# The last product of a fused retention and MoE kernel: 1024 of its 2304 tokens by Strassen's seven products

## The chip, the cores and the metric

The kernel runs on one core of one Trainium2 chip. The metric is the device time of one execution in microseconds (us). Three executions of the kernel before took 803.22, 806.06 and 806.58 us; the median is 806.06.

TensorE (PE) multiplies: a matmul holds a 128x128 stationary operand, loaded by a weight load, and streams a moving operand of up to 512 columns past it into a PSUM bank. VectorE (DVE) and ScalarE (ACT) move and combine data, and SyncE (SP) issues the DMAs, each from one queue that is worked off in order.

## The reference

```python
def _moe2_ref(x, w_in, w_out, alpha):
    h = x @ w_in
    g = np.maximum(h, 0.0) + alpha * np.minimum(h, 0.0)
    return (g @ w_out).astype(np.float32)
...
    x = np.ascontiguousarray(attn_out.transpose(0, 2, 1, 3)).reshape(B * S, H * D)   # retention
    x = _moe_ref(x=x, **moe_kwargs)                                                  # ((x w1)(x w2)) w3 w_out
    return _moe2_ref(x=x, **moe2_kwargs)
```

There are 2304 tokens (B 4 by S 576). Only the last product, g @ w_out, matters here: g is 2304 x 2048, w_out is 2048 x 512, and the result goes to `out`. The inputs' weights are float64, and everything is computed in float32.

## The kernel before

Every float32 product is made of three matmuls in fp32r, a shorter float form: an operand x is split into a high part, `hi = cast(x)` on ACT, and a low part, `lo = x - hi` on DVE (`split`, lines 172 and 173), and the product is hi·hi + hi·lo + lo·hi. Both parts of the stationary side come first with `hi`, then `lo`, so the third matmul of each three needs the low part.

The stages are, in order: retention and the two products of x (line 179), the folding of w3 with w_out (line 630), the product y (line 816), h = y @ w_in by Strassen's seven products (`Group`, line 883), and the last product (line 1044). h is made in groups (p, j): p is a pair of blocks of 384 tokens (`W`), and j one of eight (`C1`) slices of 256 of the 2048 features. Each group leaves four tiles of g, which `keep` writes to DRAM as `gd[feature block, token block]`, 128 features by 384 tokens each.

The last product reads g back. It goes in 48 steps (j, b), j a slice of 256 features and b a block of 384 tokens:

```python
steps = [(j, b) for j in range(C1) for b in range(2)] + [(j, b) for b in range(2, NB) for j in range(C1)]
```

Blocks 0 and 1 go together in six PSUM banks, because the weights w_out (`wbc`, raw pieces `raw`, line 85) become ready only during this time: `ws.tick()` moves each piece of them on through ACT and DVE (lines 93 to 116). The blocks 2 to 5 follow one after another in three banks each. A step's work:

- `load_g(n + 3)` issues two loads of 192 KB on SP's queue into a tile `gr` (a ring of three buffers, so tile n + 3 waits until the split of tile n is done, line 945).
- `split_g(n + 1)` makes `gh` on ACT and `gl` on DVE (two buffers each, so the split of step n + 1 waits until PE has finished step n - 1).
- 18 matmuls of 512 columns (line 1044), with g as the stationary operand and w_out as the moving one.
- After a block's last step, `write` copies its banks to `ot` on DVE or ACT and issues the output's DMA on SP's queue.

PE, ACT and SP work in the order in which the program is written; DVE's order is set by a scheduler when the kernel is built. Each DMA on SP's queue also waits for the DMA eight places before it.

Of the kernel before, what the change touches and what calls it, by code (L numbers as in the profile page):

```python
# [23 lines left out]
C1 = DF1 // P  # L24
# [3 lines left out]
W = 384  # L28
NB = NT // W
# [3 lines left out]
def _f32(ap):  # L33
    return ap.bitcast(F32)
# [5 lines left out]
class Steps:  # L40
# [97 lines left out]
def retention_moe_kernel(ctx: ExitStack, tc, qk, kv, w_out1, w3t, w12, w_in, w_out2, alpha, c_row, c_pair, out):  # L138
    nc = tc.nc

    def pool(stack, name, bufs=1, **kw):
        return stack.enter_context(tc.tile_pool(name=name, bufs=bufs, **kw))
# [4 lines left out]
    raws = pool(ctx, "raws", bufs=3, side="left")  # L147
    tmp = pool(ctx, "tmp", bufs=2, side="left")
# [500 lines left out]
    xo = pool(ctx, "xo", bufs=8, side="left", reuse_waits="tile")  # L649
# [4 lines left out]
    def a_sum(name):  # L654
        return sums.tile([P, 1024], F32, tag="s", name=name)
# [13 lines left out]
    def home(q, u):  # L669

        n = q % 2 * 7 + u
        if n < 8:
            return in_wa(C1 + n, f"wu{q}_{u}")
        return hold.tile([P, 2, DM], F32R, tag=f"wu{n}", name=f"wu{q}_{u}")

    class Pairs:
# [25 lines left out]
        def step(self, n, s):  # L702
            w, j = self.w, self.ORDER[n]
            q, odd = j // 2, j % 2
            i0, i1 = 2 * n, 2 * n + 1
            if s == 0:
                w.load_until(i0 + 3)
                w._first(i0)
            elif s == 1:
                w._second(i0)  # L710
                w.load_until(i0 + 4)
                w._first(i1)
            elif s == 2:
# [122 lines left out]
    py.close()  # L836


    back = pool(ctx, "back", side="right", reuse_waits="tile")
    pg = ExitStack()  # L840
    gp = pool(pg, "gp", side="right", bufs=2, reuse_waits="tile")

    def fetch(q, u):
# [20 lines left out]
    gd = {}  # L864
# [68 lines left out]
            self.product(self.b3, "S4", "B22", False)  # L933
            self.from_sum(self.b3, self.u2, 0, 1)

    NM = W // P
    steps = [(j, b) for j in range(C1) for b in range(2)] + [(j, b) for b in range(2, NB) for j in range(C1)]
    loaded, ready, accs = {}, {}, {}

    def load_g(n):  # L940
        if n < len(steps):
            j, b = steps[n]
            t = loaded[n] = gr.tile([P, 2, W], F32, tag="gr", name=f"gr{n}")
            for m in range(2):
                nc.sync.dma_start(out=t[:, m], in_=gd[2 * j + m, b])

    def split_g(n):
        if n < len(steps):
            x = loaded.pop(n)
            ready[n] = tuple(ghl.tile([P, 2, W], F32R, tag=f"g{m}", name=f"g{m}{n}") for m in "hl")  # L950
            split(ready[n][0], ready[n][1], x)

    def write(b, i):
        ot = raws.tile([P, 512], I64, tag="raw", name=f"ot{b}_{i}").bitcast(F32)[:, 0:DM]
        if i % 2:
            nc.scalar.copy(ot, accs[b][i])
# [67 lines left out]
    flush()  # L1024


    pg.close()
    used = 0
    for n, (j, b) in enumerate(steps):
# [5 lines left out]
        if b not in accs:  # L1035
            accs[b] = [bank((used + i) % 8, f"o{b}_{i}") for i in range(NM)]
            used += NM
        h, l = ready.pop(n)
        for i in range(NM):
            ic = slice(i * P, (i + 1) * P)  # L1040
            for m in range(2):
                wh, wl = wbc[2 * j + m]
                for q, (x, y) in enumerate(((h, wh), (h, wl), (l, wh))):
                    nc.tensor.matmul(accs[b][i], x[:, m, ic], y, start=(j == 0 and m == 0 and q == 0),  # L1044
                                     stop=(j == C1 - 1 and m == 1 and q == 2))
            if j == C1 - 1:
# [82 lines left out]
```

## Time and profile before

| | |
|---|---|
| three executions | 803.22, 806.06, 806.58 us |
| the profiled execution | 803.67 us, of which the span is 801.9 us |
| PE busy | 787.3 us, 98% of the span |
| DVE, ACT busy | 497.7 us (62%), 348.6 us (43%) |
| last product on PE | from 599.98 us to the end |

The stretches of the last product, by the profile's windows:

| us | PE busy | DVE busy | ACT busy | granted clock |
|---|---|---|---|---|
| 600 to 640 | 38.61 of 40 | 37.45 | 25.98 | 1.00 |
| 640 to 680 | 40.00 of 40 | 13.62 | 9.80 | 1.00 |
| 680 to 760 | 80.00 of 80 | 21.66 | 17.75 | 1.00 |
| 760 to 802 | 38.33 of 42 | 10.30 | 7.88 | 1.00 |

Busy time is time in which an instruction of the engine ran. Matmuls overlap, so a busy PE says only that it did not wait; what a matmul costs is the distance from one start to the next. The granted clock is TensorE's, 1.00 for its upper level of 2.4 GHz, 0.50 for 1.2 GHz.

### The profile page before, as it was taken

Reading aid. Unit: us, or ns where it says so; the run is one execution under the profiler, and the core shown is the slowest. Engines: PE = TensorE matmul, PEld = TensorE weight load, DVE = VectorE, ACT = ScalarE, POOL = GpSimd, SP = SyncE. Lnnn points to the kernel's source line nnn. Section 1 sums busy time; section 2 is a strip of 40 time slices with the busy share of each in tenths; the row PEclk is TensorE's granted clock in tenths of the full one; section 3 lists DMA queues with packets and bytes.
Section 4 is the critical chain, followed back from the end, with each engine's and each line's share of the span. In section 5 each row is a group of like instructions: output and inputs, shape, how many; then the busy total and the mean of one; then the engine's idle time right before and its main releaser. Section 6 shows DMA issues by size and latency. Waiting matters only on the chain.

```text
span 801.9 us, 12688 instructions
## 1 busy us (share of the span) xinstructions
PE 787.3 (98%) x4768; PEld 694.1 (87%) x4768; DVE 497.7 (62%) x895; ACT 348.6 (43%) x648; POOL 0.2 (0%) x4
## 2 busy tenths in 40 slices
PE   7999999999999999999999999999999999999998
PEld 4778888888888988999999999999987888888886
DVE  4796785325477788988843677587899933222232
ACT  3553562231255565656514465465666622222121
POOL 0000000000000000000000000000000000000000
PEclk8999999999999999999999999999999999999999
DMA  9844931571366659899916925225557635344341
GB/s 345 344 158 125 356 135 54 165 249 54 123 193 183 198 197 336 296 388 407 387 63 221 352 101 196 108 96 202 182 196 239 218 99 177 106 132 138 99 136 41
DMA packets 81341, 156.24 MB, mean 195 GB/s; under 512 B 9600, under 2 KB 57728, under 8 KB 81280
## 3 DMA queue, kind: packets, MB, share of 16 engines
q1 hardware_dynamic: 81280, 155.43, 55.7%
q8 instruction: 37, 0.61, 0.3%
q14 instruction: 24, 0.20, 0.1%
HBM read 104.02 MB, written 51.38 MB: 194 GB/s over the span
## 4 chain that ended last, share of the span: by engine, by line
PE 89%; DVE 5%; DMA 2%; ACT 1%; issue 1%; SPq 1%; ACTq 0%; DVEq 0%
PE ps L179 25%; PE o L1044 23%; PE h L883 18%; PE y L816 12%; PE pw L630 5%; PE o L342 2%; PE sc L287 2%; DMA raw<-in_w_dram 1%; PE o L333 1%; PE st L302 1%; DMA gr<-gd 0%; DVE gl L173 0%; DVE xs L349 0%; DMA xs<-x2d 0%; DVE rt L291 0%
## 5 line engine op out<-in xcount | busy, mean ns | idle before, releaser
L179 PE MATMUL ps<-xh,w 128*128 128x512 f32 (+1 forms) x640 | 186.0, 372 | 2.0 <-ACT w L112 1.6
L1044 PE MATMUL o<-wb,gh 128*128 128x512 f32 x576 | 177.6, 389 | 0.9 <-ACT gh L172 0.9
L179 PEld LDWEIGHTS ps<-xh,w 128*128 128x128 f32 x640 | 116.0, 189 | 23.6 <-ACT w L112 1.8
L1044 PEld LDWEIGHTS o<-wb,gh 128*128 128x128 f32 x576 | 108.1, 188 | 23.8 <-ACT gh L172 1.4
L179 PE MATMUL ps<-xl,w 128*128 128x512 f32 (+1 forms) x320 | 118.0, 369 | 0.0
L1044 PE MATMUL o<-wb,gl 128*128 128x512 f32 x288 | 112.3, 390 | 0.4 <-DVE gl L173 0.4
L173 DVE TENSOR_TENSOR gl<-gr,gh 128x768 fp32r<-128x768 f32 x48 | 46.0, 958 | 99.9 <-ACT gh L172 99.8
L816 PE MATMUL y<-yab,wp 128*128 128x384 f32 x576 | 100.0, 334 | 0.0
L816 PEld LDWEIGHTS y<-yab,wp 128*128 128x128 f32 x576 | 99.9, 188 | 0.1
L172 ACT CAST gh<-gr 128x768 fp32r<-128x768 f32 x48 | 40.2, 838 | 115.9 <-PE o L1044 112.6
L179 PEld LDWEIGHTS ps<-xl,w 128*128 128x128 f32 x320 | 60.4, 189 | 9.8 <-DVE xl L173 0.3
L1044 PEld LDWEIGHTS o<-wb,gl 128*128 128x128 f32 x288 | 54.1, 188 | 12.3 <-DVE gl L173 1.3
L895 DVE SCALAR_TENSOR_TENSOR g<-m,al,g 128x384 f32<-128x384 f32 x48 | 29.7, 618 | 48.9 <-ACT g L894 45.8
L883 PE MATMUL h<-xT,wv 128*128 128x384 f32 x288 | 54.9, 334 | 1.5 <-DVE g L901 1.5
L883 PE MATMUL h<-xT,wu 128*128 128x384 f32 x288 | 55.0, 335 | 0.5 <-ACT h L908 0.3
L883 PEld LDWEIGHTS h<-xT,wv 128*128 128x128 f32 x288 | 50.3, 188 | 1.8 <-DVE g L901 1.8
L108 DVE CUSTOM_DVE_ANT_0 a<-a,b 128x1024 uint16<-128x1024 uint16 x72 | 49.5, 688 | 3.5
L883 PEld LDWEIGHTS h<-xT,wu 128*128 128x128 f32 x288 | 50.2, 188 | 1.1 <-ACT h L908 0.6
L487 ACT CAST ab<-f 128x512 fp32r<-128x512 f32 (+1 forms) x40 | 23.1, 577 | 63.1 <-DVE f L491 54.5
L103 DVE TENSOR_SCALAR a<-a 128x512 f32<-128x512 f32 x72 | 30.4, 422 | 25.7 <-ACT a L93 25.4
L491 DVE TENSOR_TENSOR f<-f,ps 128x512 f32<-128x512 f32 (+1 forms) x40 | 25.3, 632 | 31.6 <-PE ps L179 31.3
L630 PE MATMUL pw<-wo,w 128*128 128x512 f32 x192 | 44.1, 390 | 0.0
(95 smaller groups left out, 1007.5 us busy)
## 6 DMA issues: line engine op xcount, KB each, us to landing
gd<-g SPq DMA_DIRECT2D x96, 192.0 KB, 1.9
gr<-gd SPq DMA_DIRECT2D x96, 192.0 KB, 2.6
abd<-ab SPq DMA_DIRECT2D x32, 512.0 KB, 4.3
raw<-in_w_out_dram SPq DMA_DIRECT2D x24, 512.0 KB, 3.7
yab<-abd SPq DMA_DIRECT2D x24, 384.0 KB, 7.9
raw<-in_w_dram SPq DMA_DIRECT2D x16, 512.0 KB, 7.1
raw<-in_w3t_dram SPq DMA_DIRECT2D x16, 512.0 KB, 4.1
rawi<-in_w_in_dram SPq DMA_DIRECT2D x16, 512.0 KB, 6.3
```

The costliest lines, as they stand in the source:

```text
L103: nc.vector.tensor_scalar(out=a, in0=a, scalar1=self.LEAST, scalar2=self.MOST, op0=ALU.max, op1=ALU.min)
L108: nc.vector.tensor_tensor(out=a.bitcast(I32), in0=a.bitcast(I32), in1=b, op=ALU.add)
L172: nc.scalar.copy(hi, src)
L173: nc.vector.tensor_tensor(out=lo, in0=src, in1=_f32(hi), op=ALU.subtract)
L179: nc.tensor.matmul(ps, a, bb, start=(n == 0), stop=(n == last))
L487: nc.scalar.copy(t[:, 0], f)
L491: nc.vector.tensor_tensor(out=f, in0=f, in1=pss[1], op=ALU.mult)
L630: nc.tensor.matmul(acc[i], a[:, ic], bb, start=(k == 0 and n == 0), stop=(k == C1 - 1 and n == 2))
L816: nc.tensor.matmul(ys[o], wpc[c][a][:, oc], yab[b, c][:, bb], start=(c == 0 and i == 0), stop=(c == C1 - 1 and i == 2))
L883: nc.tensor.matmul(ps, a[:, x, ks], b[:, y, k], start=(fresh and n == 0), stop=(n == 5), skip_group_check=True)
L895: nc.vector.scalar_tensor_tensor(out=g, in0=r, scalar=neg[:, c:c + 1], in1=g, op0=ALU.mult, op1=ALU.add)
L1044: nc.tensor.matmul(accs[b][i], x[:, m, ic], y, start=(j == 0 and m == 0 and q == 0), stop=(j == C1 - 1 and m == 1 and q == 2))
```

## The change

The 2304 tokens of the last product are divided in three. The first 1024 (blocks 0 and 1, and 256 tokens of block 2) go together in eight banks, in 24 steps (three for each j). The next 256 (the other 128 of block 2, and 128 of block 3) follow in two banks, in 16 steps of six matmuls. The last 1024 go in four rounds of 256 tokens by Strassen's seven products: for each j, g's 256 x 256 piece is four quadrants of 128 x 128 (A11 to A22) and four sums of them (S1 to S4, `add_two`), w_out's 256 x 512 piece is four quadrants of 128 x 256 and four sums (T1 to T4, `t_sums`), and seven products of three matmuls with 256 columns each take the place of eight.

```diff
-    steps = [(j, b) for j in range(C1) for b in range(2)] + [(j, b) for b in range(2, NB) for j in range(C1)]
+    TOGETHER = ((0, 0, W), (1, 0, W), (2, 0, 256))
+    THEN = ((2, 256, P), (3, 0, P))
+    steps = [(j, *x) for y in (TOGETHER, THEN) for j in range(C1) for x in y]
...
+                nc.sync.dma_start(out=t[:, m], in_=gd[2 * j + m, b][:, at:at + w])
...
+    gs = pool(ctx, "gs", side="right", bufs=3, reuse_waits="tile")
+    go = pool(ctx, "go", side="right", bufs=3, reuse_waits="tile")
...
+    def t_sums(j):
+        for m, w in enumerate((w0, w1)):
+            h, l = wbc[2 * j + m]
+            nc.vector.tensor_tensor(out=w, in0=_f32(h), in1=_f32(l), op=ALU.add)
+        less(t12[:, :HW], w0[:, HW:], w0[:, :HW])
+        less(t12[:, HW:], w1[:, HW:], t12[:, :HW])
+        def rest():
+            less(t34[:, :HW], w1[:, HW:], w0[:, HW:])
+            less(t34[:, HW:], w1[:, :HW], t12[:, HW:])
...
+            for t, cols, src in places:
+                nc.scalar.copy(t[:, 0, cols], src)
+            for t, cols, src in places:
+                nc.vector.tensor_tensor(out=t[:, 1, cols], in0=src, in1=_f32(t[:, 0, cols]), op=ALU.subtract)
...
+    def load_two(u):
+        t = sums_of[u] = gs.tile([P, 2, 7, P], F32, tag="gs", name=f"gs{u}")
+        for i in range(2):
+            j = (2 * u + i) % C1
+            for m in range(2):
+                for h in range(2):
+                    nc.sync.dma_start(out=t[:, i, PLACE[f"A{h + 1}{m + 1}"]],
+                                      in_=gd[2 * j + m, b][:, at:at + P])
...
+        for out, x, y, how in (("S1", "A21", "A22", ALU.add), ("S3", "A11", "A21", ALU.subtract),
+                               ("S2", "S1", "A11", ALU.subtract), ("S4", "A12", "S2", ALU.subtract)):
+            nc.vector.tensor_tensor(out=a[out], in0=a[x], in1=a[y], op=how)
+    def high_part(n):
+            nc.scalar.copy(x[:, 0], sums_of[n // 2][:, n % 2])
+    def low_part(n):
+            nc.vector.tensor_tensor(out=x[:, 1], in0=sums_of[n // 2][:, n % 2], in1=_f32(x[:, 0]),
...
+    ahead = [lambda: load_two(0), lambda: load_two(1), lambda: load_two(2), None, lambda: add_two(0), None,
+             lambda: high_part(0), lambda: add_two(1), lambda: low_part(0), None, lambda: high_part(1), None]
...
+        else:
+            t_steps.tick(w * 0.0032)
         load_g(n + 3)
         split_g(n + 1)
+        if n >= len(steps) - len(ahead):
+            step = ahead.pop(0)
...
+    for n in range(n_tail):
+        high_part(n + 2)
+        low_part(n + 1)
+        if n % 2:
+            add_two(n // 2 + 2)
+            load_two(n // 2 + 3)
+        for a, op, k, half in PRODUCTS:
+            for i, (y, z) in enumerate(((0, 0), (0, 1), (1, 0))):
+                nc.tensor.matmul(ps, a[:, y], b[z], start=(opens and j == 0 and i == 0),
```

After each round of eight n, six more operations on ACT and DVE combine the four banks' halves into two tiles of the output. The changed kernel's lines 947, 1092, 1102, 1107, 1112, 1146 and 1169 are the loads `gr`, the loads `gs`, the sums S, the high and the low parts `go`, the plain matmuls and those of the seven products.

**On PE**, the last rows of the program, before (o: a bank of the output; wb: a piece of w_out; gh, gl: the parts of g):

```order
L1044 MATMUL o5_2_7677<-wb14_6854,gh47_7818 128x512 x2
L1044 MATMUL o5_2_7677<-wb14_6854,gl47_7819 128x512
L1044 MATMUL o5_2_7677<-wb15_6886,gh47_7818 128x512 x2
L1044 MATMUL o5_2_7677<-wb15_6886,gl47_7819 128x512
```

and of the change (q: a bank; go: both parts of the quadrants and sums of g; t123, t4: those of the sums T):

```order
L1169 MATMUL q24_0_8359<-wb14_6845,go31_8500 128x256 x3
L1169 MATMUL q24_0_8359<-t123_7_7495,go31_8500 128x256 x3
L1169 MATMUL q24_1_8360<-t123_7_7495,go31_8500 128x256 x3
L1169 MATMUL q24_2_8361<-t123_7_7495,go31_8500 128x256 x3
L1169 MATMUL q24_2_8361<-t4_6_7391,go31_8500 128x256 x3
L1169 MATMUL q24_3_8362<-wb15_6877,go31_8500 128x256 x6
```

Each n of the last 1024 tokens is 21 matmuls of 256 columns.

**On SP's queue**, before, where step 28 of the 48 is worked on (gr: the tiles of g, two loads each):

```order
L945 DMA gr31_7347<-gd14_3_5799 128x384
L945 DMA gr31_7347<-gd15_3_5733 128x384
L945 DMA gr32_7372<-gd0_4_5761 128x384
L945 DMA gr32_7372<-gd1_4_5870 128x384
L945 DMA gr33_7397<-gd2_4_5857 128x384
L945 DMA gr33_7397<-gd3_4_5948 128x384
```

and of the change, at its step 28, the fifth of the sixteen short ones (gs: the four quadrants of two slices):

```order
L947 DMA gr31_7365<-gd6_3_5451 128x128
L947 DMA gr31_7365<-gd7_3_5404 128x128
L1092 DMA gs0_7372<-gd0_3_5217 128x128 x2
L1092 DMA gs0_7372<-gd1_3_5170 128x128 x2
L1092 DMA gs0_7372<-gd2_3_5295 128x128 x2
L1092 DMA gs0_7372<-gd3_3_5248 128x128 x2
L947 DMA gr32_7398<-gd8_2_5425 128x128
L947 DMA gr32_7398<-gd9_2_5516 128x128
```

Eight loads now stand between the loads of two steps; the same follows between gr32 and gr33 (gs1) and between gr33 and gr34 (gs2).

**On ACT**, of the change, at the end of the 24 steps of the eight banks (gh24 and gh25: the high parts of the first two short steps; ot: a copy of a finished bank; the L1065 rows: the high parts of sums T):

```order
L172 CAST gh24_7272<-gr24_7183 128x2x128
L959 COPY ot2_0_1_7291<-o2_0_1_6583 128x512
L1065 CAST t123_5_7297<-t12_5_7230 128x512
L1065 CAST t123_5_7297<-t34_5_7294 128x256
L1065 CAST t4_4_7221<-t34_5_7294 128x256
L172 CAST gh25_7307<-gr25_7235 128x2x128
```

The copy of the last bank of the eight, and three casts, stand ahead of the cast that the second short step waits for. On DVE the four sums of gs0 stand between gl31 and gl32, those of gs1 between gl32 and gl33, and those of gs2 between gl33 and gl34.

## Rows read from the trace of the kernel before

**Rows 1.** The page of the kernel before: busy time by engine, and the chain that ended last

```profile
PE 787.3 (98%) x4768; PEld 694.1 (87%) x4768; DVE 497.7 (62%) x895; ACT 348.6 (43%) x648; POOL 0.2 (0%) x4
...
PE ps L179 25%; PE o L1044 23%; PE h L883 18%; PE y L816 12%; PE pw L630 5%; PE o L342 2%; PE sc L287 2%; DMA raw<-in_w_dram 1%; PE o L333 1%; PE st L302 1%; DMA gr<-gd 0%; DVE gl L173 0%; DVE xs L349 0%; DMA xs<-x2d 0%; DVE rt L291 0%
```

**Rows 2.** The chain that ended last, its end: start us, us, what

```profile
614.88 183.46 PE o L1044 x808
...
798.36 0.69 DVE ot L958
```

**Rows 3.** PE in order of time, its 256-wide matmuls: start us, us

```profile
255.78 0.28 PE L179 MATMUL ps<-xl,w 128*128 128x256 f32 x1
...
258.06 0.40 PE L179 MATMUL ps<-xh,w 128*128 128x256 f32 x2
...
258.42 0.40 PE L179 MATMUL ps<-xh,w 128*128 128x256 f32 x2
...
278.58 0.28 PE L179 MATMUL ps<-xh,w 128*128 128x256 f32 x1
```

**Rows 4.** Groups of matmuls and weight loads by form: busy us, mean ns

```profile
L1044 PE MATMUL o<-wb,gh 128*128 128x512 f32 x576 | 177.6, 389 | 0.9 <-ACT gh L172 0.9
...
L179 PE MATMUL ps<-xh,w 128*128 128x256 f32 x128 | 23.2, 283 | 0.0
...
L1044 PEld LDWEIGHTS o<-wb,gl 128*128 128x128 f32 x288 | 54.1, 188 | 12.3 <-DVE gl L173 1.3
```

**Rows 5.** SyncE's queue in order of time, a burst of eight loads

```profile
488.13 3.64 SPq L997 DMA_DIRECT2D xs<-x2d  x8
```

**Rows 6.** SyncE's issues of the loads gr: duration ns min/median/max

```profile
L945 SPq DMA_DIRECT2D gr<-gd x96: 319/431/1068, 584.9 to 780.0; - x96
```

**Rows 7.** DMA issues: xcount, KB each, us from issue to landing

```profile
gr<-gd SPq DMA_DIRECT2D x96, 192.0 KB, 2.6
...
out_dram<-ot SPq DMA_DIRECT2D x18, 256.0 KB, 2.0
...
per_pair<-const_pair_dram SPq DMA_DIRECT2D x4, 64.0 KB, 2.2
```

**Rows 8.** SyncE's queue in order of time, two loads of 64 KB

```profile
68.08 1.06 SPq L389 DMA_DIRECT2D per_pair<-const_pair_dram  x2
```

**Rows 9.** Groups on DVE and ACT by form: busy us, mean ns

```profile
L173 DVE TENSOR_TENSOR gl<-gr,gh 128x768 fp32r<-128x768 f32 x48 | 46.0, 958 | 99.9 <-ACT gh L172 99.8
...
L116 DVE TENSOR_TENSOR wb<-a,wb 128x512 fp32r<-128x512 f32 x16 | 11.0, 685 | 0.0
...
L724 DVE TENSOR_TENSOR s<-a 128x256 f32<-128x256 f32 x8 | 3.4, 420 | 0.0
...
L172 ACT CAST gh<-gr 128x768 fp32r<-128x768 f32 x48 | 40.2, 838 | 115.9 <-PE o L1044 112.6 <-DMA gr<-gd 3.4
...
L112 ACT CAST wb<-a 128x512 fp32r<-128x512 f32 x16 | 9.9, 619 | 3.3 <-DVE a L108 3.3
...
L735 ACT CAST wu<-a 128x256 fp32r<-128x256 f32 x8 | 3.2, 406 | 0.0
...
L956 ACT COPY ot<-o 128x512 f32<-128x512 f32 x6 | 3.5, 589 | 16.8 <-PE o L1044 16.8
```

**Rows 10.** All engines in order of time, the first steps of the last product

```profile
607.41 0.69 DVE L106 SCALAR_TENSOR_TENSOR a<-raw,a 128x512 uint32<-128x512 uint32 x1
...
608.15 0.33 SPq L85 DMA_DIRECT2D raw<-in_w_out_dram  x1
...
608.54 0.90 SPq L945 DMA_DIRECT2D gr<-gd  x2
...
613.89 0.73 PE L1044 MATMUL o<-wb,gh 128*128 128x512 f32 x2 [0.95 <-ACT gh L172]
```

**Rows 11.** Granted clock (fourth column from the right) in the first stretches

```profile
8.00:12.00 4.00, 1.39 (x12) 0.78 (x10) 2.21 (x4) 1.52 (x3) 0.00 (x0) 0.82 1.03 416
...
12.00:16.00 4.00, 3.75 (x30) 3.17 (x32) 3.05 (x8) 2.35 (x5) 0.00 (x0) 0.50 1.02 415
```

More of the change, by code (lines that the diff above doesn't have):

```diff
@@ L836, in retention_moe_kernel @@
     py.close()
-    back = pool(ctx, "back", side="right", reuse_waits="tile")
     pg = ExitStack()
+    back = pool(pg, "back", side="right", reuse_waits="tile")
     gp = pool(pg, "gp", side="right", bufs=2, reuse_waits="tile")
@@ L934, in p3 @@
             self.from_sum(self.b3, self.u2, 0, 1)
-    NM = W // P
-    steps = [(j, b) for j in range(C1) for b in range(2)] + [(j, b) for b in range(2, NB) for j in range(C1)]
+    TOGETHER = ((0, 0, W), (1, 0, W), (2, 0, 256))
+    THEN = ((2, 256, P), (3, 0, P))
+    steps = [(j, *x) for y in (TOGETHER, THEN) for j in range(C1) for x in y]
     loaded, ready, accs = {}, {}, {}
@@ L941, in load_g @@
         if n < len(steps):
-            j, b = steps[n]
-            t = loaded[n] = gr.tile([P, 2, W], F32, tag="gr", name=f"gr{n}")
+            j, b, at, w = steps[n]
+            t = loaded[n] = gr.tile([P, 2, W], F32, tag="gr", name=f"gr{n}")[:, :, :w]
             for m in range(2):
-                nc.sync.dma_start(out=t[:, m], in_=gd[2 * j + m, b])
+                nc.sync.dma_start(out=t[:, m], in_=gd[2 * j + m, b][:, at:at + w])
     def split_g(n):
@@ L949, in split_g, with write @@
             x = loaded.pop(n)
-            ready[n] = tuple(ghl.tile([P, 2, W], F32R, tag=f"g{m}", name=f"g{m}{n}") for m in "hl")
+            w = steps[n][3]
+            ready[n] = tuple(ghl.tile([P, 2, W], F32R, tag=f"g{m}", name=f"g{m}{n}")[:, :, :w] for m in "hl")
             split(ready[n][0], ready[n][1], x)
-    def write(b, i):
-        ot = raws.tile([P, 512], I64, tag="raw", name=f"ot{b}_{i}").bitcast(F32)[:, 0:DM]
+    def write(b, at, i):
+        ot = raws.tile([P, 512], I64, tag="raw", name=f"ot{b}_{at}_{i}").bitcast(F32)[:, 0:DM]
         if i % 2:
-            nc.scalar.copy(ot, accs[b][i])
+            nc.scalar.copy(ot, accs[b, at][i])
         else:
-            nc.vector.tensor_copy(ot, accs[b][i])
-        t0 = b * W + i * P
+            nc.vector.tensor_copy(ot, accs[b, at][i])
+        t0 = b * W + at + i * P
         nc.sync.dma_start(out=out[t0:t0 + P, :], in_=ot)
@@ L1027, in retention_moe_kernel, with less @@
     pg.close()
+    gs = pool(ctx, "gs", side="right", bufs=3, reuse_waits="tile")
+    go = pool(ctx, "go", side="right", bufs=3, reuse_waits="tile")
+    HW = DM // 2
+    T0 = sum(w for *_, w in TOGETHER + THEN)
+    n_tail = (NT - T0) // 256 * C1
+    t123, t4, sums_of, summed, gops = {}, {}, {}, {}, {}
+    def t_sums(j):
+        w0, w1 = (tmp.tile([P, DM], F32, tag="a", name=f"w{m}_{j}", bufs=3) for m in range(2))
+        t12 = tmp.tile([P, DM], I32, tag="b", name=f"t12_{j}", bufs=2).bitcast(F32)
+        def less(out, a, b):
+            nc.vector.tensor_tensor(out=out, in0=a, in1=b, op=ALU.subtract)
+        for m, w in enumerate((w0, w1)):
[4 more added lines that the diff above has]
+        def rest():
+            t34 = tmp.tile([P, DM], I32, tag="b", name=f"t34_{j}", bufs=2).bitcast(F32)
+            less(t34[:, :HW], w1[:, HW:], w0[:, HW:])
+            less(t34[:, HW:], w1[:, :HW], t12[:, HW:])
+            t123[j] = xo.tile([P, 2, 2, W], F32R, tag="xo", name=f"t123_{j}").rearrange("p a b w -> p a (b w)")
+            if j % 2 == 0:
+                t4[j // 2] = in_wa(2 + j // 2, f"t4_{j}")
+            at = slice(j % 2 * HW, (j % 2 + 1) * HW)
+            places = ((t123[j], slice(0, DM), t12), (t123[j], slice(DM, DM + HW), t34[:, :HW]),
+                      (t4[j // 2], at, t34[:, HW:]))
+            for t, cols, src in places:
+                nc.scalar.copy(t[:, 0, cols], src)
+            for t, cols, src in places:
+                nc.vector.tensor_tensor(out=t[:, 1, cols], in0=src, in1=_f32(t[:, 0, cols]), op=ALU.subtract)
+        return rest
@@ L1028, in retention_moe_kernel @@
+    t_steps = Steps([lambda j=j, m=m: t_rest.pop(j)() if m else t_rest.update({j: t_sums(j)})
+                     for j in range(C1) for m in range(2)])
+    t_rest = {}
     used = 0
-    for n, (j, b) in enumerate(steps):
+    for n, (j, b, at, w) in enumerate(steps):
         if ws.at[3] < len(ws.pieces):
@@ L1032, in retention_moe_kernel @@
             ws.until(n_in + 2 * j + 2)
+        else:
+            t_steps.tick(w * 0.0032)
         load_g(n + 3)
         split_g(n + 1)
-        if b not in accs:
-            accs[b] = [bank((used + i) % 8, f"o{b}_{i}") for i in range(NM)]
-            used += NM
+        if n >= len(steps) - len(ahead):
+            step = ahead.pop(0)
+            if step:
+                step()
+        if (b, at) not in accs:
+            accs[b, at] = [bank((used + i) % 8, f"o{b}_{at}_{i}") for i in range(w // P)]
+            used += w // P
         h, l = ready.pop(n)
-        for i in range(NM):
+        for i in range(w // P):
             ic = slice(i * P, (i + 1) * P)
@@ L1043, in retention_moe_kernel @@
                 for q, (x, y) in enumerate(((h, wh), (h, wl), (l, wh))):
-                    nc.tensor.matmul(accs[b][i], x[:, m, ic], y, start=(j == 0 and m == 0 and q == 0),
+                    nc.tensor.matmul(accs[b, at][i], x[:, m, ic], y, start=(j == 0 and m == 0 and q == 0),
                                      stop=(j == C1 - 1 and m == 1 and q == 2))
             if j == C1 - 1:
-                write(b, i)
+                write(b, at, i)
+    t_steps.rest()
+    for n in range(n_tail):
+        j, t0 = n % C1, T0 + n // C1 * 256
+        if j == 0:
+            four = [bank((used + i) % 8, f"q{n}_{i}") for i in range(4)]
+            used += 4
+        high_part(n + 2)
[3 more added lines that the diff above has]
+            load_two(n // 2 + 3)
+        x = gops.pop(n)
+        for a, op, k, half in PRODUCTS:
+            ps = four[k][:, half * HW:(half + 1) * HW]
+            a = x[:, :, PLACE[a]]
+            b = b_operand(j, op)
+            opens = op in ("B11", "T3", "T1", "B21")
+            for i, (y, z) in enumerate(((0, 0), (0, 1), (1, 0))):
+                nc.tensor.matmul(ps, a[:, y], b[z], start=(opens and j == 0 and i == 0),
+                                 stop=(j == C1 - 1 and i == 2), skip_group_check=True)
+            if j < C1 - 1:
+                continue
+            if op == "T2":
+                e, u = (tmp.tile([P, DM], F32, tag="a", name=f"{m}{n}", bufs=3) for m in "eu")
+                ot = raws.tile([P, DM], I64, tag="raw", name=f"ot{n}").bitcast(F32)
+                nc.scalar.copy(e[:, :HW], four[0][:, :HW])
+                nc.vector.tensor_tensor(out=u[:, :HW], in0=e[:, :HW], in1=four[0][:, HW:], op=ALU.add)
+            elif op == "T3":
+                nc.vector.tensor_tensor(out=u[:, HW:], in0=u[:, :HW], in1=four[1][:, :HW], op=ALU.add)
+            elif op == "T4":
+                nc.vector.tensor_tensor(out=e[:, HW:], in0=u[:, :HW], in1=four[2][:, HW:], op=ALU.add)
+                nc.vector.tensor_tensor(out=ot[:, DM:].rearrange("p (a w) -> p a w", a=2),
+                                        in0=u[:, HW:].unsqueeze(1).to_broadcast([P, 2, HW]),
+                                        in1=four[2].rearrange("p (a w) -> p a w", a=2), op=ALU.add)
+                nc.sync.dma_start(out=out[t0 + P:t0 + 2 * P, :], in_=ot[:, DM:])
+            elif op == "B22":
+                nc.vector.tensor_tensor(out=ot[:, :DM], in0=e, in1=four[3], op=ALU.add)
+                nc.sync.dma_start(out=out[t0:t0 + P, :], in_=ot[:, :DM])
```

24 lines of the change are left out of this document (added).

## The prediction

> **What bounds the kernel now.** I read the page first: PE is busy for 98% of the span, and in the chain that ended last PE's lines make up nearly all, the last product (line 1044) 23% [rows 1]. The chain's end shows the last product without a gap: 808 matmuls in one piece of 183.46 us, then one copy and the end [rows 2]. So in this stage time is the number of matmuls by the distance between two starts, plus every time that PE waits for an operand. Two questions remain: what a 256-wide matmul costs beside a 512-wide one, and whether SP, ACT and DVE can feed the new order.
>
> **Matmuls: -6.5 us.** A 512-wide matmul costs 183.46 / 808 = 0.227 us [rows 2]. The 256-wide form is in the trace: line 179 runs it in the last 256 tokens of the first products, three in 258.42 - 258.06 = 0.36 us, and at that pace from 255.78 to 278.58 [rows 3], 0.120 us each. Its weight loads overlap (a load lasts 188 ns, more than the distance) [rows 3, 4]. Removed: 1024 tokens are 8 tiles x 16 feature blocks x 3 = 384 matmuls, 87.2 us. Added: 4 rounds x 8 slices x 21 = 672, 80.6 us. The difference is -6.5 us.
>
> The Trainium skill, "TensorE: Matmul & The Clock Gate", section "Back-to-back issue gap", gives N / 2.4 + 2.5 ns for an isolated stream, 215.8 and 109.2 ns; by that the difference would be 384 x 0.2158 - 672 x 0.1092 = 9.5 us of gain, an estimate 3.0 us better than mine. The rows show some 11 ns more per matmul at both widths, and the change has 288 matmuls more, so I keep the rows.
>
> **The opening: +1.9 us.** DVE and ACT still convert w_out here. Before, PE stood 0.95 us at step 3, because its load was issued at 608.54, behind the piece of w_out at 608.15, which waited for DVE's work of 607.41 [rows 10]. That chain does not change, but the step ahead of it shrinks from 18 matmuls to 12, so PE comes 6 x 0.227 = 1.4 us earlier to the same wait; DVE's split there is 0.27 us shorter (512 for 768 elements, [rows 9]), so +1.1. I add 0.4 each for the steps that follow the next two short ones. Bounds 0.5 and 3.
>
> **The short steps: +10.8 us.** I set T = 0 where PE ends the eighth bank's last step. A short step is 6 x 0.227 = 1.36 us. ACT or DVE starts about 0.18 us after a matmul's slot (its modelled end is 389 ns after its start, [rows 4], and the final copy starts 0.02 us after that end, [rows 2]). Back-to-back operations start some 0.08 us before the last one's end.
>
> *First wait.* The cast gh25 stands on ACT behind the copy of the last bank (0.59) and casts of 512, 256 and 256 elements (0.62, 0.41, 0.41) [rows 9]: it ends at 0.18 + 0.59 + 0.62 + 0.41 + 0.41 + 0.41 - 4 x 0.08 = 2.3. On DVE gl25 stands behind the three low parts of the same sums and one difference; the first begins at 1.35 when its cast is done, then 0.69 + 0.42 + 0.42 + 0.42 less the overlaps, so that gl25 ends at 3.4. PE, whose third matmul needs it, would have begun the step at 1.36 and in effect begins it at 3.4 - 0.45 = 2.95: 1.6 us lost. Bounds 0 and 2.
>
> *Second wait.* Three calls of `load_two` put 24 DMAs between the loads of steps 31 and 34. The tile gr31 can be loaded when gl28 is done, which needs PE to end step 26 (2.95 + 2 x 1.36 = 5.7); cast and low part bring it to 6.75. From there SP issues 30 DMAs (gr31, gs0, gr32, gs1, gr33, gs2). A burst of eight in the trace took 3.64 us, its first seven distances 0.46 each [rows 5]; the shortest issue of a `gr` load is 0.319 and the median 0.431 [rows 6]; two loads of 64 KB took 1.06 us together, 0.55 from start to start [rows 8]. I take 0.46, from the only burst of eight: the thirtieth starts at 6.75 + 29 x 0.46 = 20.1. A 64 KB load lands 2.2 us after issue [rows 7]: 22.3. DVE's four sums on gs2, each 0.42 and two of them dependent, take 1.5: 23.8. Behind them gl34, 0.42: 24.2. So step 34 begins in effect at 23.75 where undisturbed ten short steps would bring PE to 13.6: 10.1 us late, the first wait among them. The waits show at steps 32, 33 and 34 (some 2, 3 and 3 us), each behind its eight loads. With 0.39 per issue (the distance of the two SP rows in [rows 10]) it is 2.0 less, with 0.55 2.6 more.
>
> *Third wait.* The low part of go0 (896 elements, 958 + 128 x 1.05 = 1.09 us by [rows 9]) stands on DVE just ahead of gl36: 0.7. Together 10.8.
>
> **T1 to T4.** DVE's part of `t_sums` is per slice four operations of 512 or 256 elements and then five, 4.3 us, 34 us in all, over some 60 us of PE time in which only the splits of g stand beside it (0.95 us at most per step, [rows 9]). I cost it at nothing but the first wait; without that cover every us of it would be PE's.
>
> **The seven products' feed: +1.5 us.** Per two n PE needs 42 x 0.12 = 5.04 us. SP issues eight loads, 3.7 us by 0.46. DVE makes four sums and two low parts, 4 x 0.34 + 2 x 1.0 = 3.4 us; ACT two casts of 896 elements, 1.9 us. All fit, but once in eight n the outputs come between: two more DVE operations of 512 and three of 256 elements, and two DMAs on SP that wait for them, behind which the next eight loads are queued. Followed through in the order, go10, go11 and their like are ready a few tenths of a us late or early. I take 0.5 us for three of the four rounds. Bounds 0 and 5 (0.55 per issue makes SP 4.4 of 5.04 us).
>
> **The clock: +2 us.** In the trace the granted clock fell to 0.50 after a stretch in which PE worked 1.39 of 4 us, and stayed there while PE was busy 3.75 of the next 4 [rows 11]. Steps 32 to 34 are alike: 1.36 us of work, then 2 to 3 us of waiting. At the lower level a matmul takes twice as long. While PE waits anyway that costs nothing; afterwards some 4 us of work at half speed cost 2 us. Bounds 0 and 4.
>
> **The end** is unchanged: one DVE operation of 512 elements and an output DMA (2.0 us to landing, [rows 7]).
>
> **Sum.** -6.5 + 1.9 + 10.8 + 1.5 + 2.0 = +9.7 us on the profiled execution's 803.67: 813.4. The median of the runs shown is 2.4 above that execution; I say 814. All low bounds together, with 0.39 per issue: -6.5 + 0.5 + 7.2 + 0 + 0 = +1.2, 805; all high ones: -6.5 + 3 + 13.8 + 5 + 4 = +19.3, 823.
>
> **The rivals.**
>
> *The loads hide (faster).* If SP's issue of a 64 KB piece is much shorter than any row shows, the second wait goes. All other waits are 1.9 + 1.5 + 0.7 = 4.1 without the clock's, so 2.4 us are left of the gain, and the queue's delay must stay under that: 10.1 - 29 x (0.46 - p) < 2.4 gives p = 0.19 us. Below it the kernel is faster, at best by those 2.4 us and the first wait's absence: 799 to 802. For it: pieces are a third of a `gr` load's size. Against it: in [rows 5, 8] 192 KB and 64 KB loads do not differ in this direction, and no issue is below 0.319 [rows 6]. 0.13.
>
> *Small waits only (about the same).* Issues of 0.33 to 0.39 and no fall of the clock: -6.5 + 1.9 + 7 to 8.8 + 1.5 = +4 to +6 at most, with a smaller opening +2: 806 to 809. For it: 0.319 exists. Against it: those rows are issues that stood alone. 0.20.
>
> *The feed binds (much slower).* If one issue costs 0.60 or more with its waits, SP needs 4.8 us per two n and the output DMAs' waits can no longer be made up: some 2 us per round on top of the second wait's 4 more, 824 to 828. For it: [rows 8]. Against it: [rows 5]. 0.05.
>
> My own case (808 to 823) has 0.62. Within 0.5% (4 us, about what a measurement can tell from no change) means 802 to 810, and takes in the second rival and the low edge of my case. Faster 0.13, same 0.23, slower 0.64. The range 803 to 823 leaves out the gain below it and the feed above.
>
> **What the profile would show.** PE's 256-wide matmuls at 0.36 us per three in the last 80 us. In the sixteen short steps three gaps of 2 us or more, ended by line 1146's `gl` or `gh`, while SP issues eight loads of `gs` in 3.7 us each. One shorter gap near the first of them, ended by gh25. A granted clock under 1 there. I am wrong if eight loads leave SP in under 2 us, if 256-wide matmuls with these operands cost other than 0.12 us, or if PE waits in the rounds for more than 5 us in sum.

## The result, and the profile after

The changed kernel takes 815.75 us (median of four runs, 813.70 to 816.91) and the kernel before 804.76 us (four runs beside them): the ratio is 1.0117 with a 95% interval of 1.0091 to 1.0143. It is slower by 11 us. The profiled execution took 816.76 us with a span of 814.8 us, against 803.67 us and 801.9 us before.

The page of the changed kernel, with the lines that answer to [rows 1]:

```profile
PE 789.1 (97%) x5056; PEld 706.8 (87%) x5056; DVE 572.6 (70%) x1070; ACT 370.3 (45%) x697; POOL 0.2 (0%) x4
...
PE ps L179 22%; PE h L883 21%; PE y L816 12%; PE o L1146 12%; PE q L1169 8%; DMA abd<-ab 2%; SPq L1092 2%; PE o L342 2%; PE sc L287 2%; DVE a L106 1%; DMA raw<-in_w_dram 1%; PE o L333 1%; DMA raw<-in_w_out_dram 1%; PE pw L630 1%; PE st L302
```

PE has 288 matmuls more and is busy 1.8 us longer, although by the prediction the work itself should be 6.5 us shorter. A new name stands in the chain: the issue of `gs` loads on SP's queue (SPq, line 1092) with 2% of the span. The windows of the last product say where the time is (us, then busy us and count of PE, PEld, DVE, ACT and POOL, the granted clock, DMA share, GB/s): the 24 steps of the eight banks, the sixteen short steps, the four rounds.

```profile
600.00:692.00 92.00, 89.52 (x387) 73.03 (x386) 75.40 (x141) 43.28 (x75) 0.00 (x0) 0.98 0.47 154
692.00:729.00 37.00, 28.27 (x97) 20.91 (x96) 21.77 (x50) 12.29 (x28) 0.00 (x0) 0.82 0.40 117
729.00:811.00 82.00, 81.33 (x674) 80.84 (x673) 60.20 (x103) 27.84 (x33) 0.00 (x0) 1.00 0.37 110
```

The middle one is the loss: 96 matmuls at 0.227 us [rows 2] are 21.8 us of work and take 37. PE in order of time, only its rows with a wait in this stretch and the longest one of the opening (start us, us, what, and in brackets the idle time ahead and what ended it):

```profile
613.87 0.73 PE L1146 MATMUL o<-wb,gh 128*128 128x512 f32 x2 [2.02 <-ACT gh L172]
...
694.98 0.73 PE L1146 MATMUL o<-wb,gh 128*128 128x512 f32 x2 [1.28 <-ACT gh L172]
696.13 0.54 PE L1146 MATMUL o<-wb,gl 128*128 128x512 f32 x1 [0.42 <-DVE gl L173]
...
708.60 0.73 PE L1146 MATMUL o<-wb,gh 128*128 128x512 f32 x2 [1.47 <-ACT gh L172]
...
713.21 0.97 PE L1146 MATMUL o<-wb,gh 128*128 128x512 f32 x2 [2.94 <-ACT gh L172]
...
718.51 1.22 PE L1146 MATMUL o<-wb,gh 128*128 128x512 f32 x2 [2.62 <-ACT gh L172]
```

SP's queue in the same stretch, beside the burst of [rows 5]:

```profile
700.97 0.79 SPq L947 DMA_DIRECT2D gr<-gd  x2
701.81 3.75 SPq L1092 DMA_DIRECT2D gs<-gd  x8
705.65 0.85 SPq L947 DMA_DIRECT2D gr<-gd  x2
706.60 3.69 SPq L1092 DMA_DIRECT2D gs<-gd  x8
710.40 0.85 SPq L947 DMA_DIRECT2D gr<-gd  x2
711.29 3.75 SPq L1092 DMA_DIRECT2D gs<-gd  x8
715.14 6.38 SPq L947 DMA_DIRECT2D gr<-gd  x10
```

SP issues one DMA after another with hardly a pause: 700.97 to 711.29 are 22 issues in 10.32 us, 0.47 each. From the first of these rows to the last SP's own waits come to 0.5 us, and none is for an earlier DMA: these loads land 1.8 to 2.4 us after their issue, and the DMA eight places ahead was issued some 3.75 us before. PE's three large waits each end some 3 us after a pair of `gr` loads that had a burst of eight ahead of it went out (705.65, 710.40, 715.14). The casts on ACT that end them:

```profile
708.15 0.40 ACT L172 CAST gh<-gr 128x256 fp32r<-128x256 f32 x1 [3.54 <-DMA gr<-gd]
712.75 0.40 ACT L172 CAST gh<-gr 128x256 fp32r<-128x256 f32 x1 [4.20 <-DMA gr<-gd]
718.05 0.40 ACT L172 CAST gh<-gr 128x256 fp32r<-128x256 f32 x1 [4.89 <-DVE gs L1102]
```

Two of them waited for the `gr` load. The third is put down to DVE's sums on gs2, which end at that moment; its `gr` loads, issued from 715.14 on, can have landed only shortly before. The chain that ended last goes through those sums, and so through the burst of gs2:

```profile
714.14 0.43 SPq L1092
714.62 2.07 DMA gs<-gd
716.71 0.43 DVE gs L1102
...
718.51 10.95 PE o L1146 x36
```

The granted clock in the same stretch (third column from the right, in [rows 11] too, where the heading says the fourth):

```profile
692.00:696.00 4.00, 2.43 (x10) 1.38 (x8) 3.25 (x8) 2.42 (x6) 0.00 (x0) 1.00 0.82 275
696.00:700.00 4.00, 3.87 (x10) 3.06 (x11) 2.44 (x7) 0.40 (x1) 0.00 (x0) 0.57 0.36 97
...
708.00:712.00 4.00, 1.66 (x6) 0.98 (x6) 1.27 (x3) 0.40 (x1) 0.00 (x0) 1.00 0.49 137
712.00:716.00 4.00, 2.68 (x6) 1.53 (x6) 1.69 (x5) 0.40 (x1) 0.00 (x0) 0.69 0.51 137
716.00:720.00 4.00, 1.49 (x4) 1.22 (x5) 3.04 (x8) 1.95 (x6) 0.00 (x0) 0.50 0.42 110
720.00:724.00 4.00, 4.00 (x11) 3.15 (x10) 2.13 (x5) 1.53 (x3) 0.00 (x0) 0.53 0.32 90
```

From 720 to 724 PE is busy all the time and begins 11 matmuls, where at 1.00 a full window holds 18 to 20: the rest is the lower level of 1.2 GHz.

The rounds in order of time, and the wide groups of their matmuls, beside [rows 3, 4]:

```profile
769.96 1.60 PE L1169 MATMUL q<-t,go 128*128 128x256 f32 x12
771.40 1.24 PE L1169 MATMUL q<-wb,go 128*128 128x256 f32 x9
...
775.55 0.38 PE L1169 MATMUL q<-wb,go 128*128 128x256 f32 x1 [0.51 <-DVE go L1112]
```

Twelve starts in 771.40 - 769.96 = 1.44 us are 0.120 us each, as predicted, and the one wait of the 80 us is 0.51 us.

### The profile page after: what moved, and what is told of

The parts are those of the page before. It is cut to its first block, busy times and chain, and to the rows that moved or that the text cites. A ratio compares the mean times of both kernels' runs of the same rounds, so it can differ in the third digit from the quotient of the medians.

```text
span 814.8 us, 13732 instructions
## 1 busy us (share of the span) xinstructions
PE 789.1 (97%) x5056; PEld 706.8 (87%) x5056; DVE 572.6 (70%) x1070; ACT 370.3 (45%) x697; POOL 0.2 (0%) x4
## 4 chain that ended last, share of the span: by engine, by line
PE 80%; DVE 7%; DMA 6%; SPq 3%; ACT 2%; issue 2%; DVEq 0%; ACTq 0%
PE ps L179 22%; PE h L883 21%; PE y L816 12%; PE o L1146 12%; PE q L1169 8%; DMA abd<-ab 2%; SPq L1092 2%; PE o L342 2%; PE sc L287 2%; DVE a L106 1%; DMA raw<-in_w_dram 1%; PE o L333 1%; DMA raw<-in_w_out_dram 1%; PE pw L630 1%; PE st L302 1%
## 5 line engine op out<-in xcount | busy, mean ns | idle before, releaser
L1146 PE MATMUL o<-wb,gh 128*128 128x512 f32 x320 | 104.0, 407 | 10.3 <-ACT gh L172 10.3
L1146 PEld LDWEIGHTS o<-wb,gh 128*128 128x128 f32 x320 | 62.6, 197 | 25.7 <-ACT gh L172 12.7
L1146 PE MATMUL o<-wb,gl 128*128 128x512 f32 x160 | 65.3, 408 | 0.9 <-DVE gl L173 0.9
L172 ACT CAST gh<-gr 128x768 fp32r<-128x768 f32 (+2 forms) x40 | 24.8, 620 | 60.9 <-PE o L1146 37.4
L1107 ACT CAST go<-gs 128x896 fp32r<-128x896 f32 x32 | 29.4, 941 | 48.3 <-PE q L1169 20.9
L1169 PE MATMUL q<-t,go 128*128 128x256 f32 x384 | 51.3, 283 | 0.0
L1169 PEld LDWEIGHTS q<-t,go 128*128 128x128 f32 x384 | 48.4, 192 | 0.0
```

The costliest lines, as they stand in the source:

```text
L1107: nc.scalar.copy(x[:, 0], sums_of[n // 2][:, n % 2])
L1146: nc.tensor.matmul(accs[b, at][i], x[:, m, ic], y, start=(j == 0 and m == 0 and q == 0), stop=(j == C1 - 1 and m == 1 and q == 2))
L1169: nc.tensor.matmul(ps, a[:, y], b[z], start=(opens and j == 0 and i == 0), stop=(j == C1 - 1 and i == 2), skip_group_check=True)
```

## The experiments

My theory after the result: the loss is the queue of SP's issues in the short steps (24 loads of `gs` ahead of the loads that PE needs next), with a first wait ahead of it and a lower clock behind it; the seven products themselves bring about what was predicted. The rivals: the opening with eight banks, not the short steps, costs most; or the landing of the loads, not their issue; or the clock makes up most of it.

**1. The 24 loads earlier.** They are issued at steps 12, 14 and 16, where the conversion of w_out is over and the work on SP is small.

```diff
-    ahead = [lambda: load_two(0), lambda: load_two(1), lambda: load_two(2), None, lambda: add_two(0), None,
+    ahead = [None, None, None, None, lambda: add_two(0), None,
...
         split_g(n + 1)
+        if n in (12, 14, 16):
+            load_two((n - 12) // 2)
```

> The 24 loads that stood between gr31 and gr34 on SP's queue are issued 12 to 16 steps earlier, behind the loads of steps 15, 17 and 19 of the eight banks; nothing else is changed in the program's text. Theory (SP's issue time sets the second wait): the three waits at the short steps 32 to 34 and the slow clock behind them go, the first wait stays; of the 15.3 us that the short steps lose some 11 come back: 804 to 807 us. Rival (DVE's sums of g and of w_out are what the short steps wait for): the waits stay or move, at most 3 us come back: 812 to 816 us.

Measured: 803.86 us (ten runs), 0.9994 of the kernel before (0.9981 to 1.0008). PE's rows with a wait above 0.2 us in the eight banks' and the short steps (one more of 0.51 us follows in the rounds):

```profile
615.73 1.22 PE L1148 MATMUL o<-wb,gh 128*128 128x512 f32 x2 [2.20 <-ACT gh L172]
...
696.56 0.74 PE L1148 MATMUL o<-wb,gh 128*128 128x512 f32 x2 [1.43 <-ACT gh L172]
697.72 0.50 PE L1148 MATMUL o<-wb,gl 128*128 128x512 f32 x1 [0.42 <-DVE gl L173]
```

The three large waits are gone, and the clock is 1.00 in every window from 692 to 728. The same 24 issues still take 3.7 us per eight, here at 651, 657 and 664 us, of which the first:

```profile
651.03 3.76 SPq L1092 DMA_DIRECT2D gs<-gd  x8
```

So nothing about the loads changed but their place, and 11.9 us of the median went. Two things went with it. DVE's twelve sums of the quadrants, whose order the scheduler sets, moved along with the loads, to 655.4 to 671.7 us from 706.4 to 718.1, so this run alone does not part the loads from the sums; the casts shown above and experiment 2, where the sums stay, do that. And behind a first wait of the same length (1.43 and 0.42 us for 1.28 and 0.42) the clock stayed at 1.00 here, where its fall cost the changed kernel some 1.7 us; no run shows why.

**2. Four loads for eight.** Where both 128-token halves of a quadrant pair lie in one block of `gd`, one DMA of 128 KB takes the place of two of 64 KB; the bytes are the same.

```diff
+                b, at = divmod(t0, W)
+                if at + 256 <= W:
+                    first, last = (PLACE[f"A{h + 1}{m + 1}"] for h in range(2))
+                    nc.sync.dma_start(out=t[:, i, first:last + 1:last - first],
+                                      in_=gd[2 * j + m, b][:, at:at + 256].rearrange("p (h w) -> p h w", h=2))
+                    continue
```

> Both halves of a feature block come in one load of 128 KB where they lie in one block of g, so that four loads instead of eight stand between gr31, gr32, gr33 and gr34. Theory (issue count): 12 issues of 0.47 us fewer, 5.6 us back and a little of the clock's loss: 807.5 to 810.5 us. Rival (bytes, landing or DVE's sums): the same bytes and sums, 814 to 816 us.

Measured: 812.19 us (four runs), 1.0097 (1.0068 to 1.0126). The profiled execution, 811.09 us, is 5.7 us below the profiled one of the changed kernel; the medians differ by 3.6. By the median the expected size was missed; the mechanism was not: a burst of four takes half the time of one of eight, and the waits behind it shrink with it, from 1.47, 2.94 and 2.62 us to these:

```profile
707.69 0.73 PE L1152 MATMUL o<-wb,gh 128*128 128x512 f32 x2 [0.25 <-ACT gh L172]
710.75 0.73 PE L1152 MATMUL o<-wb,gh 128*128 128x512 f32 x2 [1.40 <-ACT gh L172]
713.39 0.73 PE L1152 MATMUL o<-wb,gh 128*128 128x512 f32 x2 [0.77 <-ACT gh L172]
```

and SP's queue:

```profile
702.24 1.93 SPq L1093 DMA_DIRECT2D gs<-gd  x4
704.28 0.85 SPq L947 DMA_DIRECT2D gr<-gd  x2
```

With equal bytes and half the issues, the waits of 7.03 us in sum fall to 2.42, though DVE makes the same sums in these steps (705.8 to 713.9 us) and the loads land later, 2.7 us after their issue for 2.0. It is the count of issues that held PE back, not the bytes, the landing or the sums. In the profiled executions the short steps take 30.0 us for 37.1 and the rounds 82.5 for 81.4, with a wait of 0.98 us in them. That the medians differ by less than the profiled executions is in part their choice: this one is the lowest of its four, that of the changed kernel the second highest.

**3. No T sums in steps 21 to 25**, so that ACT's three casts don't stand ahead of gh25.

```diff
-        else:
+        elif not 21 <= n <= 25:
             t_steps.tick(w * 0.0032)
```

> No step of the sums T is made during the steps 21 to 25, so that no cast of theirs stands ahead of gh25 on ACT. Theory (ACT's order makes the first wait, and all that follows is counted from it): the wait of 2.1 us at the second short step falls under 0.6, the slow clock there goes too (some 1.6 us): 812 to 814 us. Rival (SP's queue is late anyway and takes up what is saved): 815 to 816.5 us.

Measured: 813.92 us (four runs), 1.0125 (1.0090 to 1.0160). The first wait is gone; the next three, smaller than before (2.06, 2.27 and 1.71 us), begin with this one:

```profile
704.22 0.92 PE L1146 MATMUL o<-wb,gh 128*128 128x512 f32 x2 [2.06 <-ACT gh L172]
```

The short steps take 33.4 us for 37.1, but the start of the rounds now waits 0.18 and 0.63 us for `go`, behind the sums that were put off, and the rounds take 82.8 us for 81.4. The 24 steps ahead take 90.8 us for 91.9: the clock stayed at 1.00 (616 to 620 us) behind this opening wait, which the edit does not touch:

```profile
613.73 0.73 PE L1146 MATMUL o<-wb,gh 128*128 128x512 f32 x2 [2.08 <-ACT gh L172]
```

The median moved by only 1.8 us, which the two intervals do not tell from nothing.

**4. The opening alone.** Eight banks together for 1024 tokens; of the other 1280 tokens 128 follow in eight short steps with no `gs` loads among them, and the rest in blocks as before; neither seven products nor T sums.

```diff
-    THEN = ((2, 256, P), (3, 0, P))
-    steps = [(j, *x) for y in (TOGETHER, THEN) for j in range(C1) for x in y]
+    THEN = ((2, 256, P),), ((3, 0, W),), ((4, 0, W),), ((5, 0, W),)
+    steps = [(j, *x) for y in (TOGETHER, *THEN) for j in range(C1) for x in y]
...
-    T0 = sum(w for *_, w in TOGETHER + THEN)
+    T0 = NT
...
-            t_steps.tick(w * 0.0032)
+            pass
```

> The first 1024 tokens together in eight banks as in the change, but the other 1280 plainly, in one, three, three and three banks, without the seven products. Theory (the shorter third step of the opening brings PE earlier to a wait that does not move): 2 to 3 us over the kernel before in the opening and nothing later: 806.5 to 808.5 us. Rival (the eight banks cost nothing, all of the loss is in the short steps): 804 to 805.5 us.

Measured: 807.34 us (ten runs), 1.0040 (1.0024 to 1.0056). The opening's wait is 2.46 us here, and one of 0.39 us follows at 696.84, the only one in the eight short steps. So the opening costs some 3.6 us of the median (1.9 to 4.5 by the interval) and not the 11: this rival falls. Nor do short steps by themselves lose much, where neither a burst stands among their loads nor sums T beside them.

**5. The opening's wait taken away.** While w_out is converted, a step's `gr` loads go to SP's queue ahead of the next piece of w_out.

```diff
-        if ws.at[3] < len(ws.pieces):
+        early_load = ws.at[3] < len(ws.pieces)
+        if early_load:
+            load_g(n + 3)
             ws.tick()
             ws.until(n_in + 2 * j + 2)
...
-        load_g(n + 3)
+        if not early_load:
+            load_g(n + 3)
```

> While w_out is still converted, a step's loads of g are issued ahead of its piece of w_out on SP's queue, in the change and nothing else. Theory (the opening's wait is the load of step 3 behind that piece): PE's wait of 2.0 us near 614 us and the slow clock behind it go, 2 to 4 us under the change: 811 to 814 us. Rival (DVE's conversion of w_out sets that wait, whatever the queue does): 815 to 817 us.

Measured: 810.23 us (nine runs), 1.0063 (1.0039 to 1.0086), 5.5 us less than the changed kernel, and more than expected. In place of 0.21, 2.02 and 0.26 us stand 0.18 and 0.35, the latter here:

```profile
612.21 0.50 PE L1149 MATMUL o<-wb,gl 128*128 128x512 f32 x1 [0.35 <-DVE gl L173]
```

and the granted clock stays up where it had fallen to 0.82 and 0.76 in the changed kernel:

```profile
612.00:616.00 4.00, 3.79 (x17) 3.14 (x18) 4.00 (x8) 3.25 (x6) 0.00 (x0) 1.00 0.98 343
```

The 24 steps take 88.2 us for 91.9, so the wait and the clock that follows it cost 3.7. The sixteen short steps are shorter too, 34.7 us for 37.1, with waits of 1.18, 0.42, 1.83, 1.67 and 1.78 us: behind the first wait the clock stayed at 1.00 (692 to 700 us), where its fall cost the changed kernel 1.7 us. Why it stayed up is not settled.

**6. The clock alone.** Filler matmuls on w_out into a free bank, 5, 6, 12 and 11 of them ahead of the steps that wait, so that PE works through the waits. They add work that nothing reads.

```diff
+        if n in (25, 32, 33, 34):
+            x = bank(7, f"fill{n}")
+            for i in range({25: 5, 32: 6, 33: 12, 34: 11}[n]):
+                nc.tensor.matmul(x, wbc[0][0][:, 0:P], wbc[0][0], start=True, stop=True)
```

> Matmuls on w_out into an unused bank are put ahead of the short steps 25, 32, 33 and 34 (5, 6, 12 and 11 of 512 columns), in the time in which PE waits in the change; they add work and take none away. Theory (the waits also cost by the slow clock after them): the granted clock stays at 1.00 there and 2 to 5 us come back: 811 to 814 us. Rival (the clock's fall is hidden in the waits): 815 to 818 us, no gain or the price of the added matmuls.

Measured: 813.70 us (four runs), 1.0105 (1.0074 to 1.0137). The clock is 1.00 in all windows from 692 to 728, of which the one that had fallen lowest:

```profile
716.00:720.00 4.00, 3.44 (x14) 1.99 (x14) 3.51 (x9) 2.85 (x7) 0.00 (x0) 1.00 0.43 123
```

The short steps take 33.4 us for 37.1; the median is 2.05 us lower, though the two intervals overlap. The lower clock in the short steps costs 2 to 3.7 us, the rest are the waits themselves: the rival that the clock is most of the loss falls.

**7. All three repairs together:** loads at steps 12, 14 and 16 (1), no T sums in steps 22 to 25 with a rate of 0.0036 in the other steps (3), `gr` ahead of w_out's pieces (5).

> Three edits together: the 24 loads early as in the first experiment, no sums T in the steps 22 to 25, and the loads of g ahead of w_out's pieces. Theory (the waits were the whole loss, and the seven products are worth 6.5 us): the short steps lose under 1.5 us and the opening under 1.5: 797.5 to 801 us, faster than the kernel before by 0.4 to 0.8%. Rival (DVE is full in these steps and some other wait takes their place): 802 to 804 us.

Measured: 799.52 us (six runs, 798.70 to 801.40), 0.9933 of the kernel before (0.9913 to 0.9954). It beats both kernels. In the stage no wait of PE is longer than 0.6 us; the opening's are 0.20 and 0.36, the rounds' these two:

```profile
754.32 0.38 PE L1174 MATMUL q<-wb,go 128*128 128x256 f32 x1 [0.22 <-DVE go L1112]
760.19 0.38 PE L1174 MATMUL q<-wb,go 128*128 128x256 f32 x1 [0.58 <-DVE go L1112]
```

**8. The kernel before with the repair of (5) alone**, the same edit of its loop, to see what of (7) is the seven products'.

> The kernel before with the loads of g ahead of w_out's pieces, nothing else. Theory: its smaller wait at step 3 (0.95 and 0.26 us in the trace) goes: 802.5 to 803.5 us by the level of the last comparison (before 803.7), so that most of what the best version gains is not from this edit. Rival (the edit alone gives all of the gain): 800 us or less.

Measured: 801.18 us (ten runs, 800.92 to 803.09), 0.9952 (0.9933 to 0.9971), better than expected. So 3.7 of the 5.4 us by which (7) beats the kernel before come without any seven products, and 1.7 us (801.18 - 799.52, same chip; the two intervals overlap) is what they bring by the medians. In the profiled executions the last product takes 192.8 us in (7) and 196.4 us here, 3.6 less of the 6.5 that the count of matmuls gives; but it begins at 602.5 us in (7) and at 599.0 here. Over all profiled executions that start varies from 599.0 to 602.5 us, so what the seven products bring is known only roughly, 1.7 to 3.6 us.

**9. (7) with the loads of (2),** to see what sets the two waits that were left in the rounds.

> The version with early loads, the paused T sums and the gr loads ahead of w_out's piece, with four 128 KB loads in place of eight 64 KB ones where both halves lie in one block. If the two waits that were left at the start of the rounds (0.22 and 0.58 us) came from SP's issues standing ahead of the outputs' and the rounds' work, 28 issues less take them: 798.5 to 799.5 us. If VectorE and ScalarE, busy there 80 to 90% of the time, set them, the time stays at 799 to 800.5 us and the waits remain.

Measured, on another chip, where the kernel before took 804.48 us: 800.77 us (six runs, 799.67 to 801.33), 0.9952 (0.9932 to 0.9972): no gain over (7). Two waits are left in the rounds here too, at other steps and longer, 0.54 and 1.20 us, and the rounds take 83.5 us for 81.9 in (7):

```profile
768.38 0.39 PE L1180 MATMUL q<-wb,go 128*128 128x256 f32 x1 [1.20 <-DVE go L1118]
```

The DMA groups of the two kernels show what may set them, a later landing of the larger loads (KB each and us from issue to landing; first (7), then this one):

```profile
gs<-gd SPq DMA_DIRECT2D x128, 64.0 KB, 2.0
```

```profile
gs<-gd SPq DMA_DIRECT2D x48, 128.0 KB, 2.7
```

and in the chain of this one the longer landing stands ahead of the wait:

```profile
764.05 2.75 DMA gs<-gd
767.32 1.01 DVE go L1118
768.38 23.67 PE q L1180 x193
```

That SP's count of issues sets the rounds' waits is refuted: 48 issues fewer made the rounds no shorter. That the landing does is only read from this chain; no run here tried it alone, nor VectorE's load apart from it. In (7) DVE was busy for all of the 8 us that hold its two waits (753 to 761), ACT for 2.6 of them.

## Why the prediction was right, point by point

I forecast 814 us, and slower with 0.64; 815.75 came. The sum of +9.7 us on the profiled execution stands against +13.1, of which 12.1 are in the four terms, 0.3 in the stages ahead and the rest behind the last matmul and outside the span. The place of the loss, its mechanism and its largest term came as forecast; that 814 lies so near 815.75 is in part luck. The medians are 11.0 us apart, because the profiled execution before lies 1.1 us under its median and the one after 1.0 over its own; and falls of the clock that I had not counted were partly made up by terms that I had too large (0.8 us in the opening, the third wait, the rounds).

**Matmuls, -6.5 us: right.** 0.120 and 0.227 us held. By the gap that the Trainium skill gives for isolated matmuls ("TensorE: Matmul & The Clock Gate", "Back-to-back issue gap") the rounds would take 672 x 0.1092 = 73.4 us, an estimate; the rounds took 81.4 with 0.8 us lost. The measurement decides, and the row of the first products [rows 3] was the better price.

**The opening, +1.9: it was +2.5.** The chain read from [rows 10] held to a few hundredths of a us: PE begins at 613.87 where it did at 613.89 before, in a stage that started 0.28 us later, and the wait grew from 0.95 to 2.02, 1.07 us for the 1.1 forecast. The 24 steps take 91.9 us for 87.2 of work, 4.7 lost; before, 2.2 were lost in the whole stage. The 0.8 us that I added for two later steps did not come; no row of PE waits there. What I left out is the clock that fell here (0.82 and 0.76): seven matmuls from 614.86 to 617.99 take 3.13 us for 1.59. In (5), without the wait, it stayed at 1.00; in (3) it did so behind a wait of 2.08 us too, so that the wait alone does not bring it down.

**The short steps and their clock, +12.8: it was 15.3** (from 692.18 to 729.3, less 21.8). With T = 692.18:

- The first wait, 1.6 forecast, was 2.1: PE's third matmul of step 25 starts at 696.13 where step 24's end (693.54) and two matmuls make 693.99. The step at fault is that I let ACT's copy of the last bank begin at T + 0.18. It began at 692.91, T + 0.73, because its buffer `ot` was still being written out:

```profile
692.91 0.59 ACT L959 COPY ot<-o 128x512 f32<-128x512 f32 x1 [3.07 <-DMA out_dram<-ot]
693.39 1.23 ACT L1065 CAST t<-t 128x512 fp32r<-128x512 f32 x3
694.52 0.87 ACT L172 CAST gh<-gr 128x256 fp32r<-128x256 f32 x2
```

- The clock fell behind this first wait too, which I had not counted: nine matmuls from 696.13 to 699.88 take 3.75 us for 2.04, 1.7 us more, and because SP's queue waits for these steps (gr31 needs gl28), the burst starts later by about the sum. I had SP begin at T + 6.75 = 698.9; it began at 700.97.
- The burst itself, the largest term, held: from the issue of gr31 to step 34 I had 17.0 us (23.75 - 6.75), and it was 17.5 (718.51 - 700.97). An issue is 0.46 to 0.47 us, the landing 2.1, the three sums behind it 1.34 where I had 1.5 for all four. Of the three gaps of 2 us or more that I expected, the first was 1.47. Experiments 1 and 2 show its cause, the first by the place of the loads and the second by their count.
- The third wait, 0.7, did not come: no row of PE waits between 718.51 and the first `q`. PE worked there at half speed, and DVE had time.
- The clock behind step 34, 2.0, was 2.6: six steps take 10.8 us for 8.2. Experiment 6 prices all of the clock in the short steps at 2 to 3.7 us, below 2.6 + 1.7, presumably because some of what the fillers give back at step 25 is waited for at step 32.

**The rounds, +1.5: 0.8.** The range was 0 to 5 and the feed fits: eight issues take 3.7 of 5.04 us, as costed.

**T1 to T4 at nothing but the first wait:** right in the changed kernel; in (3) a small part of them shows at once where it is put off (0.18 and 0.63 us).

The rival *the loads hide* needed an issue under 0.19 us and falls with 0.47. *Small waits only* needed 0.33 to 0.39 and no fall of the clock, and falls with both. *The feed binds* needed 0.60 and falls with 0.8 us lost in the rounds. But the place of the loads matters as much as the price: with the same price per issue, (1) gives 803.86.

## What to carry to other kernels

A DMA has a price where it is issued, here back to back 0.46 to 0.48 us of one queue for each of 64, 128 and 192 KB; before work is cut into smaller pieces, count the issues that stand ahead of the load that the bottleneck needs next, and put prefetches where that queue is idle. When steps get shorter (six matmuls for eighteen), every fixed latency in the feed that the long steps hid has to be looked at again. Try the repairs on the kernel before as well: some two thirds of the final gain were there to be had without the new algorithm.

## What the runs showed of the hardware that I had not expected

- The granted clock was 0.57 from 696 to 700 us, after a stretch in which PE had worked 2.43 of 4 us, but stayed at 1.00 from 708 to 712, where it worked 1.66 of 4, and was 0.69 and then 0.50 in the next eight. Nor does the length of a wait tell: behind opening waits of 2.02 and 2.08 us the clock fell in the changed kernel and stayed at 1.00 in (3), and behind the first wait of the short steps it fell in the changed kernel and in (2) and stayed up in (1) and (5).
- The runs of the kernel before spread from 802.7 to 807.9 us (20 runs beside experiments 5 to 8), in step with a small difference in the mean granted clock: 802.7 to 805.0 in the ten runs at 0.995 and 0.996, 804.8 to 807.9 in the ten at 0.991 to 0.994. Without the opening's wait (8) they lie between 800.9 and 803.1. That this wait sometimes brings the clock down and sometimes not would explain both the spread and why its removal is worth 3.7 us where the wait was 0.95; no trace of a run near 807 us was taken, so for that kernel it is argued and not shown.
- Half as many loads of twice the size cost SP half the time but landed 0.7 us later (2.7 for 2.0 us), and in the rounds that was no gain.
